# The first pair's Gram writes, its inverse's write and its first unit's read-back are begun by ScalarE instead of SyncE

## The chip, the core and the metric

The kernel runs on one core of a Trainium2 chip. The core has a matrix engine (TensorE, PE in the profile, with PEld for its weight loads), a vector engine (VectorE, DVE), an engine for activations and copies (ScalarE, ACT), a general engine (GpSimd, POOL) and an engine that only starts transfers (SyncE, SP). Transfers between the memory outside the core (DRAM in what follows) and the core's own memory are DMAs. SP, ACT and POOL can begin one; in the profile the queues of those engines are SPq, ACTq and POOLq. Every engine works through its own list of instructions in order.

The metric is the time of one execution on the device in microseconds (us), the median over runs.

## What is computed

Two stages run one after the other. The first is a recurrence over 768 time steps for 4 batches and 8 heads with vectors of 48 elements; the second is a layer with a cosine gate on the 3072 x 384 result.

```python
k_n = k / (np.linalg.norm(k, axis=-1, keepdims=True) + 1e-06)
state = np.zeros((B, H, D, D))
for t in range(S):
    y[:, :, t] = einsum('bhd,bhde->bhe', q[:, :, t], state)
    v_old = einsum('bhde,bhd->bhe', state, k_n[:, :, t])
    state = state + beta[:, :, t] * einsum('bhd,bhe->bhde', k_n[:, :, t], v[:, :, t] - v_old)
x = y.transpose(0, 2, 1, 3).reshape(B * S, H * D)      # 3072 x 384
h = x @ w_in                                           # w_in 384 x 2048
out = (h * cos(h)) @ w_out                             # w_out 2048 x 384
```

The reference's w_in and w_out are handed over in double precision; the kernel makes float32 of them itself.

## The kernel before

**Units and pairs.** The 768 steps are cut into 24 units of 32 steps (`NU`, `C`). Within a unit the recurrence is solved at once: a Gram matrix of the keys is formed for each batch and head (32 x 32), a triangular matrix made from it is inverted, and the inverse is applied to v less what the state already yields. Two units make a pair, m = 0 to 11, since 2 units x 8 heads x 4 batches = 64 matrices, each split in two shares, fill the 128 partitions for the inversion.

**The path of one pair.** For a unit n, PE transposes k and q (`turn`, tile p_t), ACT copies the result to kq_t (`turn_out`, L572), PE forms the Gram products p_g (`gram`, L593), and DVE scales the half that holds the keys into g (`gram_keys`, L604) and masks the other into tt (L613). `gram_put` (L620 to L633) writes g to DRAM as g_dr, one DMA for each of the first 8 units, three for later ones. When both units of a pair are written, `gram_get` (L640) reads them back in another layout as gb. `invert` (L669 and L676, one pair of instructions for a column) computes the inverse z: for pair 0 on DVE in a tile of the matrix engine's output memory, for all later pairs on POOL. For pair 0 ACT copies it out (`invert_out`, L680). `put` (L683 to L687) writes z to DRAM as z_dr, in 128-byte rows, and `get` (L689 to L694) reads it back for one unit as zt with four DMAs, one for each batch.

**Use of the inverse.** PE multiplies zt with the right side (`solve`, L742, p_u), DVE scales the result to u (`solve_out`, L752), PE forms the update of the state from u (`update`, L765, p_s), DVE adds it to the state st (L775 for unit 0, L773 later), and PE forms the unit's output (`within`, L782) and the products of the next unit with the state (`through_state`, L711). ACT copies the output to y (L793), PE transposes it (p_z, L801), ACT copies it to x_ffn (L809). Then the second stage runs on it: `hidden` (L822), later `layer` (L938), the gate on ACT and DVE, and `output` or `product` (L964, L1021).

**Weights.** w_in comes in 12 tiles, w_out in 16. Each is loaded by SP as pairs of 32-bit words (L462, tile pairs, 512 or 384 KB), split on ACT (L470 and L472), shifted on DVE (L476 and L481) and added on POOL (L485). The text counts the tiles t0, t1 and so on in the order of loading; t0 to t11 are those of w_in. The first hidden products need t0 to t2, the fourth t9 to t11. Further work on DVE that the text names: `norms_sum` (L502), `scale` (L525 to L533, after POOL's pow, L514), `weigh` (L550, the tile vp that holds v), `in_sums` (L915), `right_side` (L726, rhs).

**Order.** The order of the work is not that of the source. A planner, class `Order`, takes every task with an engine, an estimated cost, its dependences and a due time, plays the schedule through, and writes the instructions down in that order; at the end of the function each instruction is pinned behind the one before it on its engine. A task is planned on the engine that its entry names: `gram_put`, `put` and `get` are entered as tasks of SP, whoever begins the DMA in the end.

**Waits of DMAs.** The compiled program has eight completion semaphores for the DMAs that SP and ACT begin. They are handed out in turn over both engines' DMAs in the planner's order, and a DMA waits until the one that had the same semaphore before it has landed.

Of the kernel before, what the change touches and what calls it, by code (L numbers as in the profile page):

```python
# [248 lines left out]
def kernel(  # L249
# [32 lines left out]
    nc = tc.nc  # L282
# [31 lines left out]
    def half(i):  # L314
        return slice(DP * i, DP * i + DP)
# [4 lines left out]
    def quarter(b):  # L320
        return slice(C * b, C * b + C)
# [78 lines left out]
    for b in range(B):  # L400
        nc.gpsimd.dma_start(
            out=bq[C * b : C * b + H].rearrange("p n t -> p (n t)"), in_=beta[b]
# [80 lines left out]
    def narrow_add(t):  # L483
# [4 lines left out]
    sums, squares, scales, kq_ts, p_ts, p_gs, gs, grams, gbs, z_drs, zs, zts = (  # L488
        {} for _ in range(12)
    )  # L490
# [129 lines left out]
    def gram_put(n):  # L620
        m = n // 2
        if m not in gbs:
            gbs[m] = dram.tile([2, H, B, C, C], FP, name="g_dr")
        g, g_dr = gs.pop(n), gbs[m][n % 2]
        parts = [(slice(0, 128), slice(0, H), slice(0, B))]
        if n >= PLAIN_TURNS:
            parts = [(slice(0, 128), slice(0, H, 2), slice(0, B))] + [
                (half(i), slice(1, H, 2), slice(2 - 2 * i, 4 - 2 * i)) for i in range(2)
            ]
        for rows, heads, bs in parts:  # L630
            nc.sync.dma_start(
                out=g_dr[heads, bs].rearrange("h b j i -> (b j) h i"), in_=g[rows, heads]
            )  # L633

# [47 lines left out]

    def put(m):  # L683
        z_drs[m] = dram.tile([ROWS, SPLIT, 2, H, B, C], FP, name="z_dr")
        nc.sync.dma_start(
            out=z_drs[m].rearrange("r s u h b i -> (s u h b) r i"), in_=zs.pop(m)
        )  # L687

    def get(n):  # L689

        zts[n] = work.tile([128, H, C], FP, name="zt")
        z_dr = z_drs[n // 2].rearrange("r s u h b i -> u b (r s) h i")[n % 2]
        for b in range(B):
            nc.sync.dma_start(out=zts[n][quarter(b)], in_=z_dr[b])  # L694


    p_kqs, rhss, p_us, us, p_ss, ys, p_zs = ({} for _ in range(7))
# [407 lines left out]
    def inverse(m):  # L1105
        add(("gram_get", m), "SP", 1.2, lambda: gram_get(m),
            [("gram_put", 2 * m), ("gram_put", 2 * m + 1)], makes=[("gb", ("gb", m))],
            uses=[("g_dr", m)], moves=1.6)
        held = VECTOR.get(m)
        z = ("p_i", m) if held else ("z", m)  # L1110
        add(("eye", m), "ACT", 0.65, lambda: invert_eye(m, held),
            [("gram_put", 2 * m + 1)] + ([("eye", m - 1)] if m else []),
            makes=[(held or "z", z)])
        deps = [("eye", m), ("gram_get", m)]
        ends = [0, 4, 8, 12, 16, 20, 24, C - 1]
        for i, (x, y) in enumerate(zip(ends, ends[1:])):
            each = (0.2, 0.001) if held else (0.323, 0.00178)
            cost = sum(
                2 * (each[0] + each[1] * (j // SPLIT + 1) * (C - 1 - j)) for j in range(x, y)
            )  # L1120
            add(("inv", m, i), "DVE" if held else "POOL", cost,
                lambda x=x, y=y: invert(m, held, range(x, y)), deps,
                uses=[("gb", m)] if y == C - 1 else [])
            deps = [("inv", m, i)]
        if held:
            add(("inv_out", m), "ACT", 0.65, lambda: invert_out(m), deps,
                makes=[("z", ("z", m))], uses=[z])
            deps = [("inv_out", m)]
        add(("put", m), "SP", 0.45, lambda: put(m), deps, makes=[("z_dr", ("z_dr", m))],
            uses=[("z", m)], moves=1.7)  # L1130

    def unit(n):
# [47 lines left out]
        else:  # L1180
# [15 lines left out]
        add(("gram_queries", n), "DVE", 0.46, lambda: gram_queries(n), [("gram_keys", n)],  # L1196
            uses=[("p_g", n)])
        add(("gram_put", n), "SP", 0.45 if n < PLAIN_TURNS else 1.35, lambda: gram_put(n), [("gram_keys", n)],
            makes=[] if second else [("g_dr", ("g_dr", m))], uses=[("g_gram", n)],
            moves=0.85)  # L1200
        if second:
            inverse(m)
        add(("get", n), "SP", 1.9, lambda: get(n), [("put", m)], makes=[("zt", ("zt", n))],
            uses=[("z_dr", m)], moves=0.9)

# [275 lines left out]
```

## Time and profile before

| What | Value |
|---|---|
| time, median of 3 runs | 674.22 us (672.86 to 675.32) |
| the profiled execution, its own time | 676.74 us |
| its span, first to last instruction | 675.0 us |
| granted clock of TensorE | 0.99 |
| PE busy | 612.4 us (91%) |
| DVE busy | 475.6 us (70%) |
| POOL busy | 348.8 us (52%) |
| ACT busy | 295.5 us (44%) |
| DMA queue q1 (begun by SP) | 212964 packets, 49.98 MB, 39.0% of 16 engines |
| DMA queue q10 (begun by ACT) | 2176 packets, 0.39 MB, 0.4% |

The profile is one execution; its span is cut into 40 slices of 16.9 us for the rows of digits, in which 9 means busy for 90% or more. A line of a timeline gives the start in us from the start of the span, the duration, the engine, the line of the kernel, the operation, the tile written and the tile read, how many instructions are merged, and in brackets the idle time before it with what ended it. A line of waits gives who waited for whom, the sum in us, how often, and the longest. The chain of waits is followed back from the last instruction to what released each. In this kernel the chain runs through PE for 85% of the span, through DMA and POOL for 4% each.

### The profile page before, as it was taken

What the parts mean: (1) busy time and instruction counts of PE and PEld (TensorE: products, weight loads), DVE (VectorE), ACT (ScalarE), POOL (GpSimd) and SP (SyncE); (2) the same over time, 40 slices, a digit from 0 to 9 for tenths busy, and PEclk for the clock granted to TensorE, in tenths of its full rate; (3) what the DMA queues carried; (4) which work ended last, traced back from release to release, by engine and by line L of the source; (5) the groups of instructions that cost most, each with busy time, mean ns of one, the idle gap of its engine ahead of it and who ended that gap; (6) DMA issues with size and microseconds to landing.
All of it is one profiled execution on the core that took longest, in us unless ns stands there. A gap on an engine that the chain in (4) does not pass through costs nothing.

```text
span 675.0 us, 27309 instructions
## 1 busy us (share of the span) xinstructions
PE 612.4 (91%) x11864; PEld 573.0 (85%) x11864; DVE 475.6 (70%) x912; ACT 295.5 (44%) x510; POOL 348.8 (52%) x734
## 2 busy tenths in 40 slices
PE   4303798999999999999999999999999999999996
PEld 3203787896899989999999999999999989999996
DVE  5899488877576776886876876776766656656661
ACT  4432367572144452653543453544444434435530
POOL 4469888876858317678276384482382680000000
PEclk9999798999999999999999999999999999999999
DMA  8897766365462362443534524515213203000000
GB/s 179 193 197 169 165 141 166 84 104 90 68 100 54 58 106 52 71 82 59 110 42 62 108 39 66 106 26 90 57 21 53 59 3 57 1 5 24 1 24 24
DMA packets 215516, 52.56 MB, mean 78 GB/s; under 512 B 206948, under 2 KB 210164, under 8 KB 215396
## 3 DMA queue, kind: packets, MB, share of 16 engines
q1 hardware_dynamic: 212964, 49.98, 39.0%
q8 instruction: 93, 1.52, 1.0%
q10 hardware_dynamic: 2176, 0.39, 0.4%
q0 software_dynamic: 256, 0.44, 0.3%
q14 instruction: 27, 0.22, 0.1%
HBM read 39.76 MB, written 11.01 MB: 75 GB/s over the span
## 4 chain that ended last, share of the span: by engine, by line
PE 85%; DMA 4%; POOL 4%; issue 3%; SPq 2%; ACT 1%; DVE 1%; ACTq 0%; POOLq 0%; DVEq 0%
PE p_h L938 29%; PE p_out L1021 28%; PE p_h L822 6%; PE p_kq L711 4%; PE p_u L742 3%; PE p_s L765 3%; PE p_out L964 3%; PE p_kq L782 3%; PE p_g L593 2%; DMA kp<-in_k_dram 2%; PE p_o L1021 2%; PE p_z L801 1%; POOL knrm L514 1%; POOL w_in L485 1%; POOL part L669 1%
## 5 line engine op out<-in xcount | busy, mean ns | idle before, releaser
L669 POOL TENSOR_TENSOR part<-z,gb 128x126 f32<-128x126 f32 (+22 forms) x341 | 135.5, 397 | 109.4 <-DMA gb<-g_dr 44.9
L676 POOL TENSOR_TENSOR z<-z,part 128x126 f32<-128x126 f32 (+22 forms) x341 | 138.6, 406 | 26.7
L938 PE MATMUL p_h<-x_ffn,w_in 128*128 128x128 f32 x1120 | 143.6, 277 | 0.2 <-DVE g_ffn L957 0.2
L938 PEld LDWEIGHTS p_h<-x_ffn,w_in 128*128 128x128 f32 x1120 | 135.3, 192 | 1.9 <-DVE g_ffn L957 0.5
L1021 PE MATMUL p_out<-w_out,g_ffn 128*128 128x192 f32 x672 | 123.6, 329 | 1.6 <-issue 1.6
L1021 PEld LDWEIGHTS p_out<-w_out,g_ffn 128*128 128x128 f32 x672 | 107.6, 190 | 2.8 <-issue 1.7
L862 ACT ACTIVATE turns<-p_h 128x512 int32<-128x512 f32 x96 | 57.0, 595 | 101.3 <-DVE p_h L957 73.5
L1021 PE MATMUL p_out<-w_sum,g_ffn 128*128 128x192 f32 x496 | 91.6, 329 | 0.0
L874 ACT ACTIVATE turns<-turns 128x512 f32<-128x512 f32 x96 | 60.4, 630 | 46.2 <-DVE turns L867 46.1
L1021 PEld LDWEIGHTS p_out<-w_sum,g_ffn 128*128 128x128 f32 x496 | 79.3, 190 | 0.9
L867 DVE SCALAR_TENSOR_TENSOR turns<-p_h,turns 128x512 f32<-128x512 f32 x96 | 65.6, 684 | 17.6 <-ACT turns L862 17.2
L878 DVE TENSOR_TENSOR g_ffn<-turns,p_h 128x512 f32<-128x512 f32 x96 | 65.4, 681 | 17.9 <-ACT turns L875 17.0
L1037 DVE TENSOR_TENSOR g_ffn<-g_ffn 128x512 f32<-128x512 f32 x88 | 63.2, 719 | 13.2 <-PE p_out L1021 12.6
L514 POOL TENSOR_TENSOR knrm<-ksum,halves 128x16 f32<-128x16 f32 (+1 forms) x14 | 36.7, 2628 | 65.9 <-DVE ksum L502 65.9
L875 ACT ACTIVATE turns<-turns,halfpi 128x512 f32<-128x512 f32 x96 | 69.3, 722 | 3.1
L957 DVE TENSOR_TENSOR p_h<-g_ffn,p_h 128x512 f32<-128x512 f32 x60 | 41.7, 696 | 38.7 <-PE p_h L938 34.2
L954 ACT COPY g_ffn<-p_h 128x512 f32<-128x512 f32 x60 | 35.0, 583 | 74.2 <-PE p_h L938 73.9
L822 PE MATMUL p_h<-x_ffn,w_in 128*128 128x128 f32 x384 | 47.9, 283 | 0.6 <-POOL w_in L485 0.6
L822 PEld LDWEIGHTS p_h<-x_ffn,w_in 128*128 128x128 f32 x384 | 45.5, 196 | 2.0 <-POOL w_in L485 0.8
L1071 DVE SCALAR_TENSOR_TENSOR o<-p_out,o 128x192 f32<-128x192 f32 x74 | 25.2, 353 | 27.6 <-PE p_out L1021 25.2
L938 PE MATMUL p_h<-x_sum,in_sum 128*128 128x128 f32 x320 | 43.7, 280 | 0.0
L938 PEld LDWEIGHTS p_h<-x_sum,in_sum 128*128 128x128 f32 x320 | 39.5, 191 | 1.1
(95 smaller groups left out, 783.7 us busy)
## 6 DMA issues: line engine op xcount, KB each, us to landing
pairs<-in_moe_w_in_dram SPq DMA_DIRECT2D x12, 512.0 KB
gb<-g_dr SPq DMA_DIRECT2D x24, 256.0 KB
pairs<-in_moe_w_out_dram SPq DMA_DIRECT2D x16, 384.0 KB
vp<-in_v_dram SPq DMA_DIRECT2D x96, 48.0 KB
out_dram<-o SPq DMA_DIRECT2D x23, 192.0 KB
z_dr<-z SPq DMA_DIRECT2D x12, 256.0 KB
zt<-z_dr SPq DMA_DIRECT2D x96, 32.0 KB
kp<-in_k_dram SPq DMA_DIRECT2D x128, 24.0 KB
```

The costliest lines, as they stand in the source:

```text
L514: nc.gpsimd.tensor_tensor(out=scales[m][2][:, part], in0=sums[m, part.start][:, 0:n], in1=halves[:, 0:n], op=ALU.pow,)
L669: eng.tensor_tensor(out=part, in0=z[:, 0:rows, j, None].to_broadcast(shape), in1=a[:, j, None, j + 1 :].to_broadcast(shape), op=ALU.mult,)
L676: eng.tensor_tensor(out=behind, in0=behind, in1=part, op=ALU.subtract)
L822: nc.tensor.matmul(p_h[:, i], w_in[:, t, (4 * k + i) * 128 : (4 * k + i + 1) * 128], xts[p][:, t, unit * 128 : (unit + 1) * 128], start=(t ...
L862: nc.scalar.activation(turns[p, f], hidden_of(p, f), AF.Copy, scale=TURN)
L867: nc.vector.scalar_tensor_tensor(out=r, in0=hidden_of(p, f), scalar=TURN, in1=t, op0=ALU.mult, op1=ALU.subtract,)
L874: nc.scalar.activation(r, r, AF.Abs)
L875: nc.scalar.activation(r, r, AF.Sin, bias=halfpi, scale=-2.0 * math.pi)
L878: nc.vector.tensor_tensor(out=place(p, f), in0=step_of(rests.pop((p, f)), f), in1=step_of(hidden_of(p, f), f), op=ALU.mult,)
L938: nc.tensor.matmul(p_h[:, e], in_sum[:, odd_tile, 4 * s + e] if a == "s" else w_in[:, a, f * 128 : (f + 1) * 128], x_sums[p][:, unit] if b ...
L1021: nc.tensor.matmul(p_o, left(p, part, a)[:, e % 4], right(e, b), start=(e == 0), stop=(e == FT // 2 - 1), skip_group_check=True,)
L1037: nc.vector.tensor_tensor(out=left(p, s, to), in0=left(p, s, one), in1=left(p, s, two), op=op)
```

## The change

Three calls that began a DMA on SyncE begin it on ScalarE where the pair is the first (m is 0) or, for the read-back, where the unit is the first (n is 0). These are seven DMAs: g of units 0 and 1 (128 KB each), z of pair 0 (256 KB), and zt of unit 0 (four of 32 KB). The read of gb, the read-back for unit 1 and all later pairs stay on SyncE.

```diff
@@ gram_put @@
         for rows, heads, bs in parts:
-            nc.sync.dma_start(
+            (nc.sync if m else nc.scalar).dma_start(
                 out=g_dr[heads, bs].rearrange("h b j i -> (b j) h i"), in_=g[rows, heads]
             )
@@ put @@
         z_drs[m] = dram.tile([ROWS, SPLIT, 2, H, B, C], FP, name="z_dr")
-        nc.sync.dma_start(
+        (nc.sync if m else nc.scalar).dma_start(
             out=z_drs[m].rearrange("r s u h b i -> (s u h b) r i"), in_=zs.pop(m)
         )
@@ get @@
         for b in range(B):
-            nc.sync.dma_start(out=zts[n][quarter(b)], in_=z_dr[b])
+            (nc.sync if n else nc.scalar).dma_start(out=zts[n][quarter(b)], in_=z_dr[b])
```

The planner's entries are unchanged, so the order of PE, DVE and POOL stays as it was. On ACT the seven DMAs stand at the places that the planner's order gives them:

| ACT's list, after | Then |
|---|---|
| split of t1 (L470, L472) | g_dr of unit 0, then the two copies to kq_t of unit 2 (L572), then g_dr of unit 1, then ksq (L497) |
| split of t7 | z_dr |
| split of t8 | the four zt of unit 0, then the split of t9 |

On SP they are gone from between the other DMAs, which keep their order. The semaphores are handed out anew over the planner's order: z_dr has the place between the third and the fourth of the k loads that SP begins at 43.80 us, and the four zt stand between the q and v loads that SP begins at 49.35 and 53.84 us.

## Prediction

> **What bounds the kernel now.** First the page: the span and the row of TensorE (PE) by slices of 16.9 us.
>
> ```profile
> span 675.0 us, 27309 instructions
> ...
> PE   4303798999999999999999999999999999999996
> ...
> DMA  8897766365462362443534524515213203000000
> ```
>
> From about 75 us on PE is full, so only the moment at which it starts its dense part counts. PE is busy 612.4 us by the page; of its 62.6 idle us only about 7 lie after 75 us, by its waits. The waits of PE before 70 us name the last obstacle, and those from 75 to 130 us show how little slack comes after it:
>
> ```profile
> PE p_u L742 <- DMA zt<-z_dr: 25.4, 1, 25.4
> ...
> PE p_h L822 <- POOL w_in L485: 0.6, 1, 0.6
> ```
>
> PE waits 25.4 us for zt of unit 0, the read-back of the first pair's inverse. The timeline of SyncE's queue (SP) shows how that read comes about:
>
> ```profile
> 48.38 0.39 SPq L462 DMA_DIRECT2D pairs<-in_moe_w_in_dram  x1
> 48.87 0.39 SPq L685 DMA_DIRECT2D z_dr<-z  x1
> 49.35 4.45 SPq L369 DMA_DIRECT2D qp<-in_q_dram  x4
> 53.84 1.93 SPq L369 DMA_DIRECT2D vp<-in_v_dram  x4
> 55.87 0.39 SPq L462 DMA_DIRECT2D pairs<-in_moe_w_in_dram  x1
> 56.31 4.13 SPq L694 DMA_DIRECT2D zt<-z_dr  x8
> 60.54 0.40 SPq L462 DMA_DIRECT2D pairs<-in_moe_w_in_dram  x1
> ```
>
> By the landing events of the trace the write of z_dr lands at 54.06, yet zt is begun at 56.31: SP has four q loads, four v loads and a weight load to issue first. The first four zt land at 60.40 to 60.95. So far an earlier zt looks like a gain of 3 us. VectorE (DVE) says otherwise, because the step after p_u is its u (L752):
>
> ```profile
> 59.91 0.68 DVE L915 TENSOR_TENSOR in_sum<-w_in 128x512 f32<-128x512 f32 x1
> 61.40 0.69 DVE L476 SCALAR_TENSOR_TENSOR pairs<-pairs 128x512 uint32<-128x512 uint32 x1 [0.81 <-ACT pairs L472]
> 62.01 0.42 DVE L481 TENSOR_SCALAR w_in<-w_in 128x512 uint32<-128x512 uint32 x1
> 62.51 1.02 DVE L752 TENSOR_TENSOR u<-p_u,bz 128x384 f32<-128x384 f32 x2
> ```
>
> In DVE's order the shift of weight tile t9 stands ahead of u and ends at 62.43, while p_u ends at 62.47: two chains arrive together. The shift waits for ScalarE (ACT), and ACT for the weight load that SP began at 55.87 and that landed at 60.13:
>
> ```profile
> 47.47 0.69 ACT L470 ACTIVATE w_in<-pairs 128x512 f32<-128x512 f32 x1 [1.33 <-DMA pairs<-in_moe_w_in_dram]
> ...
> 52.48 0.67 ACT L470 ACTIVATE w_in<-pairs 128x512 f32<-128x512 f32 x1 [3.75 <-DMA pairs<-in_moe_w_in_dram]
> ...
> 60.15 0.67 ACT L470 ACTIVATE w_in<-pairs 128x512 f32<-128x512 f32 x1 [6.45 <-DMA pairs<-in_moe_w_in_dram]
> ```
>
> One more thing is needed, the waits of SP's queue from 44 to 66 us:
>
> ```profile
> SPq L694 <- DMA pairs<-in_moe_w_in_dram: 0.4, 1, 0.4
> ```
>
> A read of zt waits for a weight load with which it shares no data. It is the eighth zt, the eighth DMA after that load: begun at 60.14, 0.01 after the load landed. Eight completion semaphores are handed round over all DMAs of SP and ACT together, and each DMA waits until the one eight places ahead has landed. I call them lanes.
>
> **What the Trainium skill says.** "DMA: Bandwidth & Descriptors", Issuing engines are not separate DMA queues: all issuers share the same 16 DMA engines, so a second issuer saves issue time only. The trace bears on this with DMA busy 7 to 9 tenths until 84 us. Queues, rings and completion order there gives SP and ACT a ring each, served in turn by packets: a write on ACT's ring need not stand behind SP's loads. No run here shows how the two share. Anatomy of one DMA adds that semaphores are waited for on the issuing sequencer, before dispatch; the eighth zt agrees, and SP's next load at 60.54 stood behind it.
>
> **The change part by part.** It moves 7 DMA issues (two g_dr, one z_dr, four zt of unit 0) from SP to ACT; no arithmetic changes.
>
> *Gram writes.* On SP they took 0.40 and 0.54 us at 17.79 and 18.29. On ACT one stands ahead of the copies of kq_t at 17.05, one behind them; ACT's q loads at the start took 0.32 to 0.47 us each, so about 0.9 us is added there. Behind them is ksq at 18.22, which DVE reads at 19.91; it ended at 18.74, so 1.17 us of slack cover the 0.9. If that failed, the pow of POOL at 20.53 and everything behind it would slip by the rest. The lanes move too: one write takes a place ahead of the last k load of unit 3, one ahead of its q loads, so the last three q loads wait for lanes that land at 15.90, 16.23 and 17.71, and the third weight load begins about 18.1 instead of 16.95. It lands 1.2 us later; the fourth unit's Gram product follows at about 24.2 to 25.4, and its consumer on DVE stands at 25.86: covered by 0.4. The read gb waits for both writes; on their own ring they land earlier than 22.39, but 1 MB of weights still stands ahead of gb. I take DVE's inverse to start at 27.4 as now, between 0.4 earlier (DVE is free at 26.95) and 1 us later; later it is hidden by the 0.81 us that DVE waits at 60.6 and by the point below. Cost 0, bounds 0 and +1.
>
> *Write of z.* z is ready on ACT at 46.15, but the issue stands behind the split that runs 47.47 to 48.73: begun at 48.75, against 48.87. Landing: now 54.06 behind a weight load; a z_dr issued alone at 237.34 took 3.26 us. So 52.0 to 54.1; I take 53.3. SP loses an issue and the stall of 2.97 us that its next q load shows at 49.35, but the second of those q loads (52.37 now) has the lane that z_dr holds, eight places on: it waits until 53.3.
>
> *Reads of zt.* On ACT behind the split of tile t8: load landed 52.45, split ended 53.71. So zt is begun at 53.8, 54.25, 54.7, 55.2. Undisturbed zt take 1.8 to 2.0 us (at 202 to 205 us); they land at 55.8, 56.3, 56.8, 57.3, some 3.6 us earlier than now, and p_u ends near 59.3.
>
> *What is late next.* SP now issues the q load at 53.3, its next at 53.7, 54.15, then v at 54.65; the second v waits for the q load of 53.3 to land (55.4), the third at 55.8, the fourth for the first zt (56.2), and the load of t9 for the second zt, eight places ahead: about 56.6 instead of 55.87. A weight load takes 3.9 to 4.3 us (4.25 for this one): landed at 60.8, +0.7. Split, shift and u follow with the same gaps as now (60.13 to 62.51, 2.38): u at 63.2, +0.7. p_u is long done. DVE's earlier wait for v (weighing at 57.92, its last v landed at 57.55, then at 58.5) ends 0.6 later and fits in the wait ahead of the shift.
>
> *To the end.* p_s follows u by 1.17; state, features and the first hidden product (75.18) follow without a wait on anything that stands still: the gap of 2.94 at 68.48 is an issue gap inside PE and moves along. POOL's 0.6 at 91 depends on weight loads that SP issues after v of the next pair, which wait for DVE's rhs, so it moves too. The whole 0.7 reaches the end. Span 675.0 + 0.7 = 675.7; with the 1.74 outside it (676.74 less 675.0) 677.4 for a profiled execution. That one lay 2.5 above the median of 674.22; on the median the forecast is 674.9.
>
> **The rivals.**
> A. No harm at t9, and the early zt counts (0.08). Then DVE is free at 60.59, its shift ends at 61.6, u at 61.7: at most 0.8 gained, 673.4. For it: p_u no longer holds u. Against: t9's lane. To beat 0.3% (2.02 us; about what this measurement can tell from no change) something else must help too, such as two fuller rings in the first 50 us; 0.06.
> B. Slower (0.27): the two rings share the engines between 48.8 and 54, so the load of t8, now landed ahead of z_dr, lands up to 1.5 later, at 54. ACT's split stands ahead of zt and ends at 55.3; the second zt lands at 57.8, t9 begins at 58, lands at 62.2, u is 2.1 late: 676.3, with the zt themselves at 3 us 677.4. It decides above 0.3% from a second zt landing after 57.8. For it: DMA busy 9 and 7 tenths in the slices to 50.6 and 67.5 us. Against: the load is issued 0.4 ahead of z_dr.
> C. The Gram writes cost more (inside B's chance for a third): an issue of over 0.6 us each on ACT, or gb over 1.9 later; +1 to +2 on its own, 675.5 to 676.5.
> D. That nothing happens, since the reads land too late in either kernel: ruled out by the order on ACT, which leaves zt over 2 us earlier.
>
> **How the numbers follow.** The forecast (t9 later by 0.3 to 1.6) has 0.6, A 0.08, B and C 0.27, a clear gain 0.05. Predicted 674.9; the forecast's own range with the spread of the median, 0.8, is 673.8 to 676.4. To leave no more than 2 in 10 out, 673.0 to 677.6. Faster 0.06, same 0.65, slower 0.29.
>
> **What would show it.** In the changed profile: ACT issues g_dr near 17.1 and 18.5, z_dr near 48.8, four zt from 53.8; PE's p_u begins between 55.8 and 57.4; its wait for DVE's u grows from 1.2 to about 4; t9 begins at 56.3 to 57.5 and ACT splits it at 60.5 to 61.5; the first hidden product starts near 75.9. Wrong if u stays at 62.5 or earlier, if gb on DVE starts after 28.5, or if the gap at 68.48 vanishes.

## The result, and the profile after

Over 12 runs each, the changed kernel took 675.24 us (median, 672.37 to 680.11) and the kernel before 675.09 us (671.92 to 678.81). The ratio is 1.0003, its 95% interval 0.9978 to 1.0028: no difference that can be measured. Run again beside the experiments below, it was 1.0008 (0.9985 to 1.0031). Of all timed executions here one, of r6 below, took 1710.73 us and does not count in its ratio.

The page of the changed kernel, span and rows by slices of 16.8 us:

```profile
span 672.6 us, 27309 instructions
...
PE   4302898999999999999999999999999999999996
...
PEclk9999699999999999999999999999999999999999
```

PE becomes dense in the same slice as before, the fifth. The timeline of the queues and of ACT shows the moved DMAs where the prediction had put them:

```profile
48.33 0.67 ACT L470 ACTIVATE w_in<-pairs 128x512 f32<-128x512 f32 x1 [1.70 <-DMA pairs<-in_moe_w_in_dram]
48.39 0.39 ACTq L685 DMA_DIRECT2D z_dr<-z  x1
48.89 0.66 ACT L472 ACTIVATE pairs<-pairs 128x512 uint32<-128x512 uint32 x1
49.23 0.40 SPq L462 DMA_DIRECT2D pairs<-in_moe_w_in_dram  x1
49.73 4.05 SPq L369 DMA_DIRECT2D qp<-in_q_dram  x4
53.96 3.20 SPq L369 DMA_DIRECT2D vp<-in_v_dram  x4
53.97 0.67 ACT L470 ACTIVATE w_in<-pairs 128x512 f32<-128x512 f32 x1 [4.42 <-DMA pairs<-in_moe_w_in_dram]
54.03 0.83 ACTq L694 DMA_DIRECT2D zt<-z_dr  x2
54.53 0.66 ACT L472 ACTIVATE pairs<-pairs 128x512 uint32<-128x512 uint32 x1
54.90 0.96 ACTq L694 DMA_DIRECT2D zt<-z_dr  x2
...
57.44 0.35 SPq L462 DMA_DIRECT2D pairs<-in_moe_w_in_dram  x1
```

The read-back of zt begins at 54.03 instead of 56.31, and t9's load (the last line) at 57.44 instead of 55.87. The waits of SP's queue from 44 to 60 us say why t9's load is later:

```profile
SPq L369 <- DMA z_dr<-z: 2.0, 1, 2.0
SPq L369 <- DMA zt<-z_dr: 1.6, 1, 1.6
...
SPq L462 <- DMA zt<-z_dr: 0.2, 1, 0.2
```

A q load waits for z_dr, a v load for the first zt, t9's load for the second zt. None shares data with what it waits for; they share completion semaphores, handed round over SP's and ACT's DMAs together. VectorE's timeline shows the end of that chain, and PE's waits what it costs there:

```profile
62.71 0.69 DVE L476 SCALAR_TENSOR_TENSOR pairs<-pairs 128x512 uint32<-128x512 uint32 x1 [1.24 <-ACT pairs L472]
63.32 0.42 DVE L481 TENSOR_SCALAR w_in<-w_in 128x512 uint32<-128x512 uint32 x1
63.65 1.01 DVE L752 TENSOR_TENSOR u<-p_u,bz 128x384 f32<-128x384 f32 x2
```

```profile
PE p_s L765 <- DVE knrm L525: 5.4, 1, 5.4
```

The profile names the instruction next to u on DVE as the releaser; in r4 below it names u. Of that wait at most 1.24 us, the idle time ahead of the shift, is due to t9's load; most of the rest is DVE's own work, as r5 and r8 below show. p_u now starts at 56.97 and ends near 59.4, and PE then stands 5.4 us until u is there (1.2 before). The early read-back bought a longer wait.

### The profile page after: what moved, and what is told of

Read it like the earlier page. It is cut to its first block, busy times and chain, and to the rows that moved or that the text cites. A ratio compares the mean times of both kernels' runs of the same rounds, so it can differ in the third digit from the quotient of the medians.

```text
span 672.6 us, 27309 instructions
## 1 busy us (share of the span) xinstructions
PE 612.6 (91%) x11864; PEld 573.3 (85%) x11864; DVE 474.4 (71%) x912; ACT 295.5 (44%) x510; POOL 346.4 (52%) x734
## 3 DMA queue, kind: packets, MB, share of 16 engines
q10 hardware_dynamic: 7408, 1.05, 1.0%
q8 instruction: 93, 1.52, 1.0%
## 4 chain that ended last, share of the span: by engine, by line
PE 80%; DMA 8%; SPq 3%; POOL 2%; DVE 2%; issue 2%; ACT 1%; ACTq 0%; POOLq 0%
PE p_h L938 29%; PE p_out L1021 27%; PE p_h L822 5%; PE p_kq L711 4%; PE p_out L964 3%; PE p_s L765 3%; PE p_u L742 3%; PE p_kq L782 2%; PE p_g L593 2%; DMA pairs<-in_moe_w_in_dram 2%; POOL knrm L514 2%; DMA kp<-in_k_dram 2%; DMA zt<-z_dr 2%; PE p_o L1021 2%; DMA z_dr<-z 1%
## 5 line engine op out<-in xcount | busy, mean ns | idle before, releaser
L676 POOL TENSOR_TENSOR z<-z,part 128x126 f32<-128x126 f32 (+22 forms) x341 | 136.9, 402 | 26.7
L822 PE MATMUL p_h<-x_ffn,w_in 128*128 128x128 f32 x384 | 48.9, 288 | 0.4 <-issue 0.4
L822 PEld LDWEIGHTS p_h<-x_ffn,w_in 128*128 128x128 f32 x384 | 46.5, 201 | 1.7 <-POOL z L676 0.7
```

The lines of the kernel that those rows point to most:

```text
L676: eng.tensor_tensor(out=behind, in0=behind, in1=part, op=ALU.subtract)
L822: nc.tensor.matmul(p_h[:, i], w_in[:, t, (4 * k + i) * 128 : (4 * k + i + 1) * 128], xts[p][:, t, unit * 128 : (unit + 1) * 128], start=(t ...
```

## The experiments

All, r1 to r12 for short, compute the same. All but r4, r7 and r8 reorder the planner's tasks; r4 is the changed kernel as it is, r7 and r8 are the two parts of the change. The edit is nine lines in class `Order` and a table: a task named in the table is written only after the task it is held behind, and the rest keeps its order.

```diff
+    HOLD = {task: the task that it is held behind}
+    def write(self, key, emit, makes, wrote, seen=set(), held={}):
+        if self.HOLD.get(key, key) not in seen | {key}:
+            held.setdefault(self.HOLD[key], []).append((key, emit, makes))
+            return
+        emit()
+        wrote([tag for tag, _ in makes])
+        seen.add(key)
+        [self.write(k, e, t, wrote) for k, e, t in held.pop(key, ())]
...
-                emit()
-                wrote([tag for tag, _ in makes])
+                self.write(key, emit, makes, wrote)
```

One table of marks serves for all of them: one profiled execution of each kernel, us from the start of its span, and the ratio to the kernel before from timed runs made beside it. "t11 ready" is the end of t11's add on POOL (L485); the p_out is the first of L964; "later p_h" is the hidden product of L822 that comes first after the second group of p_out. An issue gap, in what follows, is idle time of an engine in which it waited for nothing that the profile shows.

| Kernel | u | first p_h | t11 ready | first p_out | later p_h | ratio (95%) |
|---|---|---|---|---|---|---|
| before | 62.51 | 75.18 | 90.98 | 93.69 | 117.75 | 1 |
| changed | 63.65 | 75.44 | 91.37 | 95.10 | 117.92 | 1.0003 (0.9978 to 1.0028) |
| r1 | 59.13 | 74.39 | 91.33 | 94.04 | 113.73 | 0.9981 (0.9964 to 0.9997) |
| r2 | 61.73 | 76.65 | 91.51 | 94.23 | 118.15 | 1.0033 (1.0017 to 1.0048) |
| r3 | 65.56 | 76.34 | 91.41 | 94.12 | 116.02 | 1.0030 (1.0013 to 1.0047) |
| r4 | 62.00 | 73.43 | 89.57 | 92.63 | 115.42 | 1.0008 (0.9985 to 1.0031) |
| r5 | 60.81 | 75.75 | 90.86 | 93.92 | 117.39 | 1.0016 (0.9997 to 1.0035) |
| r6 | 61.95 | 75.46 | 90.61 | 93.58 | 115.82 | 1.0007 (0.9980 to 1.0034) |
| r7 | 62.69 | 75.49 | 91.27 | 93.99 | 117.85 | 1.0014 (0.9997 to 1.0032) |
| r8 | 62.36 | 73.67 | 90.13 | 92.84 | 115.46 | 1.0011 (0.9995 to 1.0028) |
| r9 | 61.93 | 77.21 | 93.33 | 96.22 | 117.67 | 1.0029 (1.0014 to 1.0045) |
| r10 | 61.06 | 72.52 | 90.44 | 93.16 | 115.25 | 1.0016 (0.9991 to 1.0040) |
| r11 | 61.60 | 74.88 | 90.36 | 93.07 | 115.08 | 1.0000 (0.9983 to 1.0018) |
| r12 | 58.42 | 73.32 | 86.57 | 92.98 | 115.63 | 1.0004 (0.9986 to 1.0023) |

**r1 and r2: does what stands ahead of u eat the early zt?** On DVE, the weighing of v, the copies of beta, in_sum, the shift of t9 and a scale go behind the copy of st (`update_out`), and on PE a Gram product goes later; r2 is the same on the kernel before.

```diff
+    HOLD = {("weigh", 1): ("update_out", 0), ("beta_home",): ("update_out", 0), ("in_sums", 3, 0): ("update_out", 0),
+            ("shift", 9): ("update_out", 0), ("scale", 2, 0): ("update_out", 0), ("gram", 4): ("state", 1)}
```

> The changed kernel, with u of unit 0 (and the state copy after it) taken ahead of the work that DVE had in front of it: the weighing of v, the copies of beta, in_sum, the shift of t9 and the scale of pair 2; on PE the Gram product of unit 4 goes behind the state product of unit 1. Theory (the early zt is lost because u stands behind the shift of t9, which waits for a weight load tied to the zt by the semaphores): u starts within 0.3 us of the end of p_u, at 59 to 60.5 instead of 63.65; the first hidden product starts near 72 instead of 75.4. Whether the end gains is then set by POOL: its adds of t6 to t11 end near 85 to 91 whatever PE does, so PE waits 2 to 4 us for w_in and at most 1.1 us reaches the end (about 674). Rival (nothing else holds PE back): the whole 3 to 3.5 us reach the end, about 671.5, with no wait of PE for POOL. Second rival (u was not held by t9): u stays later than 62.

> The same moves on DVE and PE in the kernel before, as the control. Theory: p_u ends at about 62.5 there, so u cannot start before and stays at 62.4 to 62.7; the first hidden product within 1 us of 75.2, the time within 0.3% of before. Rival (the moves themselves are worth something or cost something): over 2 us away from before in either direction.

With the list cleared, u follows p_u in the changed kernel by 0.03 us: 59.13, which is 4.5 us ahead of the changed kernel's first profile and 2.9 ahead of its second, r4. That half of the theory is shown. The first hidden product, expected near 72, gained only 1.05 us on the first profile and none on r4 (73.43). PE's waits of r1 from 40 to 140 us name what came instead:

```profile
PE p_kq L711 <- ACT y L793: 3.1, 1, 3.1
PE p_z L801 <- DVE tt L613: 2.1, 1, 2.1
PE p_h L822 <- POOL w_in L485: 1.9, 2, 1.2
PE p_s L765 <- DVE u L752: 1.2, 1, 1.2
```

ACT's copy of y stands behind the splits of t9 and t10 and a ksq; DVE's tt stands behind the work that was moved. The control r2 is slower by 0.33%, a little more than its theory allowed, so the moves cost time by themselves; r1 is 0.52% better than its control, and 0.19% better than the kernel before.

**r3: is PE's dense part bound by u at all?** In the kernel before, zt of unit 0 is read only behind t10's load.

```diff
+    HOLD = {("get", 0): ("weights", 10)}
```

> The kernel before with the four reads of zt for unit 0 behind those for unit 1 and the load of t10 on SP. They are begun near 59 instead of 56.3 and land near 63 to 64; u starts near 65 instead of 62.5. Theory (from u on, nothing stands still that could take up a delay): the end comes 2 to 3 us later, about 677. Rival (a wait later on, such as POOL's adds, takes it up): within 1 us of before.

u came 3.05 us later and the first hidden product 1.2 later, since the issue gap on PE that was 2.94 us shrank to 0.88. t11 and the first p_out came 0.4 later. The timed runs lost 0.30%, 2.0 us, which fits the theory. That it was the lateness of u which reached the end is not shown: the profile loses most of it on the way, and r2 lost as much with u 0.8 earlier than in the kernel before.

**r4: the changed kernel again.**

> The changed kernel once more. Theory: t9's load on SP begins within 0.1 us of the landing of the second zt, SP's second q load of that group within 0.1 us of the landing of z_dr, u 0.5 to 1.5 us later than 62.5, and the time within 0.3% of before. Rival (the single profile was an accident): t9 begins before the second zt has landed, or u at 62.5 or earlier.

The waits are the same (p_s 5.3 us for u; SP 2.1 for z_dr, 1.2 and 0.2 for zt), yet u stands at 62.00 and the first hidden product at 73.43, 2.0 earlier than in the first profile of the same kernel. z was copied at 45.05 here, at 46.04 there: single executions of one kernel differ by a microsecond before the write of z and the reads of zt are even reached. By the rival (u at 62.5 or earlier), and by the prediction's own sign of being wrong, this execution speaks against a late u; the two waits through shared semaphores stand in it as forecast.

**r5 and r6: t9's load alone.** The four q loads ahead of t9's load are begun behind it; r6 is the kernel before with the same edit.

```diff
+    HOLD = {("q", 6): ("weights", 9)}
```

> The changed kernel with one edit on SP: the four q loads that stood ahead of the four v loads and of t9's load are begun behind t9's load. PE, DVE, ACT and POOL keep their order, u still stands behind the shift of t9. Theory (the late load of t9 on SP is what eats the early zt): t9's load is begun near 53.5 instead of 57.4 and lands near 57.5 to 58; its split on ACT ends near 59.2, its shift on DVE near 60.2, so u starts near 60.2 to 60.6 instead of 62.0 to 63.65, PE's wait for u falls from 5.3 to about 2, and two thirds of some 2.5 us reach the end: ratio 0.9975 (0.9965 to 0.9985). Rival (DVE's own list, the weighing and in_sum, holds u, or the traffic of q behind t9 slows the read-back): u stays at 61.5 or later, ratio 0.999 to 1.002.

> The kernel before with the same edit on SP, as a control. Theory: t9's shift is then early (near 60), but the read-back of zt keeps its place behind v, t9 and q on SP, p_u ends near 62.5 as before, and u follows it: ratio 1.000 (0.9985 to 1.0015). Rival (an early t9 is worth something by itself, through POOL's adds or SP's later loads): ratio below 0.9985.

u moved to 60.81 in r5, as the theory said, and the wait ahead of t9's shift (1.24 us in the changed kernel, 0.89 in r4) is gone. But the rival is right in part. PE's wait for u fell to 2.07, but at least half of that because p_u ended later, 15.09 us after the start of z's copy (13.37 in the changed kernel, 12.81 in r4); and no wait was left ahead of u on DVE from z's copy on, yet u came 16.0 us after it. The same holds for r8 below, in which t9's load was not moved and PE waited 5.0 us for u. VectorE's timeline of r8 has no bracket ahead of u, so no wait:

```profile
60.82 0.68 DVE L915 TENSOR_TENSOR in_sum<-w_in 128x512 f32<-128x512 f32 x1
61.42 0.69 DVE L476 SCALAR_TENSOR_TENSOR pairs<-pairs 128x512 uint32<-128x512 uint32 x1
62.02 0.42 DVE L481 TENSOR_SCALAR w_in<-w_in 128x512 uint32<-128x512 uint32 x1
62.36 1.02 DVE L752 TENSOR_TENSOR u<-p_u,bz 128x384 f32<-128x384 f32 x2
```

So DVE's own work between z's copy and u takes some 16 us (15.7 to 16.2 in the six profiles without a wait there: r5, r6 and r8 to r11), and t9's load only adds its wait to that. r1, which takes work away, has 13.2.

The time of r5 did not follow (1.0016; the control 1.0007). In its timelines of SP, ACT and PE:

```profile
60.16 1.47 SPq L462 DMA_DIRECT2D pairs<-in_moe_w_in_dram  x1
...
65.59 0.68 ACT L470 ACTIVATE w_in<-pairs 128x512 f32<-128x512 f32 x1 [7.53 <-DMA pairs<-in_moe_w_in_dram]
...
67.67 0.46 ACT L793 COPY y<-p_kq 128x384 f32<-128x384 f32 x1
...
68.18 1.79 PE L711 MATMUL p_kq<-st,kq_t 48*32 48x48 f32 x128 [1.31 <-ACT y L793]
```

What was taken from t9 was given to t10: its load ended late, ACT split it at 65.59, and y, behind that split, held PE. A further issue gap of 3.41 us stood ahead of the second p_u.

**r7 and r8: the change in its two parts,** the Gram writes alone and the rest alone.

```diff
-            nc.sync.dma_start(
+            (nc.sync if m else nc.scalar).dma_start(
                 out=g_dr[heads, bs].rearrange("h b j i -> (b j) h i"), in_=g[rows, heads]
```

This is r7, against the kernel before; r8 has the two other parts of the change's diff and not this one.

> The kernel before with only the two Gram writes of the first pair on ACT. Theory (this part costs nothing and gives nothing that lasts): gb on DVE is read between 26.9 and 28.4, the later chain stands as before, zt on SP near 56.3, u near 62.5; ratio 1.000 (0.9985 to 1.0015). Rival 1 (the late third and fourth weight loads push the inverse): DVE's inverse starts at 28 or later and all behind it moves by 0.7 to 1: ratio 1.001 to 1.0015. Rival 2 (the writes on their own ring bring gb early): inverse starts at 26.9, ratio 0.999 to 0.9995.

> The kernel before with only the write of z and the read-back of unit 0 on ACT, the Gram writes on SP. Theory (all that the change does about u is in this part): zt begun near 53.5 on ACT, p_u from 55.5 to 57, t9's load begun 0.7 to 1.2 later than 55.87, u at 62.3 to 63.6 behind t9's shift, PE waits 5 us for u: ratio 1.000 (0.999 to 1.0015). Rival (the Gram part had cost what this part gave): u at 61.7 or earlier, ratio 0.997 to 0.9985.

In r7 DVE's inverse started at 27.76 after a wait of 0.50 for gb (27.38 and 0.44 before) and u at 62.69; in r8 zt was begun at 53.12, t9's load at 56.35, u at 62.36, with 5.0 us of PE's wait for it. Neither ratio differs from 1 or from the other's: no large gain in one part is hidden by a loss in the other.

**r9, r10, r11: the walls behind u.** r9 is r5 with y ahead of t10's split; r10 clears the path of units 0 and 1 on all engines; r11 is r10's control, on the kernel before.

```diff
+    HOLD = {("q", 6): ("weights", 9), ("split", 10): ("within_out", 0), ("square", 3, 0): ("within_out", 0), ("shift", 10): ("split", 10)}
```

```diff
+    HOLD = {("q", 6): ("weights", 9), ("split", 10): ("within_out", 0), ("square", 3, 0): ("within_out", 0), ("shift", 10): ("right", 1),
+            ("sum", 3, 0): ("right", 1), ("scale", 2, 0): ("update_out", 0), ("gram", 4): ("features_out", 0), ("gram_keys", 4): ("gram", 4),
+            ("gram_queries", 4): ("gram_keys", 4), ("gram_put", 4): ("gram_keys", 4), ("split", 11): ("features_out", 0), ("shift", 11): ("split", 11),
+            ("inv", 1, 6): ("add", 8), ("put", 1): ("inv", 1, 6), ("add", 12): ("add", 10), ("add", 13): ("add", 12)}
```

> The changed kernel with t9's load ahead of the q loads (as in r5_after_t9_early) and, on ACT, y of unit 0 ahead of the split of t10 and the ksq behind it. Theory (in r5_after_t9_early the wall behind u was t10's load, which began 1.5 late and held y in ACT's list): u near 60.8, y near 65.1 instead of 67.67, PE's wait for y (1.31) gone, the p_kq of unit 1 near 66.9 instead of 68.18, the first hidden product 1.3 earlier than 75.75, ratio 0.9985 to 1.000. Rival (the issue gap of 3.41 inside PE takes up what comes early): first hidden product at 75.3 or later, ratio as in r5_after_t9_early, 1.001 to 1.002.

> r9_after_y_first, and further moves on the path of units 0 and 1: on DVE st of unit 0 ahead of the scale of pair 2, rhs of unit 1 ahead of the shift of t10; on PE gram of unit 4 behind p_z; on ACT the split of t11 behind x_ffn; on POOL the adds of t7 and t8 ahead of the last part of pair 1's inverse, and those of t9 and t10 ahead of the first two of w_out. Theory (each of these stood on the path behind the early zt): u near 60.8, p_kq of unit 1 near 65.6, rhs near 67.4, first hidden product between 71 and 74 (70.9 and an issue gap), no wait for POOL's w_in above 0.5; ratio 0.995 to 0.998. Rival (POOL is the bound behind it: the later z_dr of pair 1, or w_in's adds, take the gain back between 80 and 100 us): first hidden product at 72 to 74, new waits of PE of 2 us or more on POOL or on zt of unit 2, ratio 0.9985 to 1.002.

> The kernel before with the same moves as r10_after_full, as its control. Theory (the early zt is worth its time only where nothing stands behind it): p_u ends near 62.5 and u follows at once, so every step to the first hidden product is 1.7 to 2 later than in r10_after_full; ratio 0.15 to 0.3 per cent above that of r10_after_full. Rival (an issue gap of PE or POOL's work sets the start of the dense part in either kernel): both ratios agree within 0.1 per cent.

r9 is a miss of the theory: PE's wait for y vanished, but issue gaps of 2.27 and 3.03 us stood in its place, the first hidden product came at 77.21, and the ratio is 1.0029. r10's first hidden product came where the theory had it, at 72.52, 2.4 ahead of its control, but not through u: 0.9 of the 2.4 stands already at z's copy (44.90 and 45.80), 1.46 is an issue gap that the control has just before 71.41 and r10 lacks, and counted from z's copy u is no earlier (16.16 and 15.80). The timed runs do not bear the theory out: the control was to be slower by 0.15% to 0.3% and measured 1.0000 against 1.0016. And r10's first p_out stands at 93.16, the control's at 93.07. Ahead of it lie, in r10's timeline of PE,

```profile
81.95 0.89 PE L765 MATMUL p_s<-u,kp 64*64 64x96 f32 x32 [1.71 <-ACT kq_t L572]
...
90.49 2.50 PE L822 MATMUL p_h<-x_ffn,w_in 128*128 128x128 f32 x20 [1.06 <-POOL w_in L485]
```

and the second is the more general. In r10 t11 was ready at 90.44, and PE started at 90.49. The same pair of rows in the kernel before, first PE's timeline, then POOL's:

```profile
91.03 2.50 PE L822 MATMUL p_h<-x_ffn,w_in 128*128 128x128 f32 x20 [0.64 <-POOL w_in L485]
```

```profile
89.36 1.62 POOL L485 TENSOR_TENSOR w_in<-w_in,pairs 128x512 uint32<-128x512 uint32 x1
```

89.36 and 1.62 make 90.98; PE started 0.05 later. In ten of the kernels (before, r1, r2, r3, r5, r7 to r11) this product began 0.05 to 0.06 us after t11 was ready, with the first hidden product anywhere from 72.5 to 77.2. PE waited only 0.2 to 1.1 us there, r10 1.06 where its control waited 0.27. POOL was busy for 9.9 to 10.0 of the 11 us from 80 to 91 in before, r1 and r10, mostly on adds. Its list is a second clock that u doesn't set: counted from z's copy, u comes after 13.2 us in r1, 17.0 in the kernel before and 19.8 in r3, and t11 is ready after 45.4, 45.4 and 45.6.

**r12: take that wall away,** in the kernel that was fastest. r1 with the adds of three tiles of w_out behind the add of t11.

```diff
+            ("add", 12): ("add", 11), ("add", 13): ("add", 11), ("add", 14): ("add", 11)}
```

> r1_after_u_early with one edit more, on POOL: the adds of the first three tiles of w_out stand behind the add of t11 instead of between the adds of t7 to t11. Theory (the first hidden products need t9 to t11 at about 90 us whatever comes before, and in nearly every kernel the fourth of them starts within 0.06 us of the end of t11's add on POOL, so POOL's list is what eats an earlier start): t11's add ends near 87.5 instead of 91.3, both waits of PE for POOL's w_in (1.22 and 0.64 in r1_after_u_early) vanish, the first p_out starts near 92.3 instead of 94.04, ratio 0.9955 (0.994 to 0.997). Rival (the next wall stands directly behind it: the adds of w_out, that p_out needs, end as late as before, or DVE's turns and rhs come no earlier): p_out at 93.5 or later, ratio 0.9975 to 0.999.

POOL's timeline, then PE's, of r12:

```profile
79.44 7.13 POOL L485 TENSOR_TENSOR w_in<-w_in,pairs 128x512 uint32<-128x512 uint32 x5
86.53 3.40 POOL L485 TENSOR_TENSOR w_out<-w_out,pairs 128x384 uint32<-128x384 uint32 x3
```

```profile
87.58 1.22 PE L711 MATMUL p_kq<-st,kq_t 48*32 48x48 f32 x110 [0.86 <-issue]
...
92.62 0.52 PE L801 MATMUL p_z<-consts,y 128*128 128x128 f32 x3 [0.49 <-DVE tt L613]
92.98 2.75 PE L964 MATMUL p_out<-w_out,g_ffn 128*128 128x384 f32 x8
```

t11 was ready at 86.57, 4.8 us earlier than in r1, and both waits for POOL are gone, as the theory said. The first p_out gained 1.06 over r1, but this execution's first hidden product was 1.07 earlier already: issue gaps and DVE's tt stand where POOL's waits (1.86 us together) were. The ratio is 1.0004, so for the time the theory falls. In this profile the rival's picture fits, a next wall directly behind POOL's, though its numbers (p_out at 93.5 or later, a ratio below 1) were not met.

**Where r1's profile gains.** At its first p_out, r1 is 0.35 later than the kernel before, so the lead of its profile does not come from the early u as such. It comes between 107 and 114 us. PE's timelines, the kernel before, then r1:

```profile
109.12 0.66 PE L562 MATMUL p_t<-consts,kp 128*128 128x128 f32 x4
112.08 1.02 PE L562 MATMUL p_t<-consts,qp 128*128 128x128 f32 x4 [2.30 <-issue]
112.89 4.12 PE L964 MATMUL p_out<-w_out,g_ffn 128*128 128x384 f32 x8
```

```profile
109.31 0.66 PE L562 MATMUL p_t<-consts,kp 128*128 128x128 f32 x4
109.80 0.60 PE L562 MATMUL p_t<-consts,qp 128*128 128x128 f32 x4
110.24 2.75 PE L964 MATMUL p_out<-w_out,g_ffn 128*128 128x384 f32 x8
```

All other profiles have an issue gap of 0.7 to 2.3 us among these transposes; r1 has none. In the kernel before the clock was halved after it as well: eight p_out took 4.12 us instead of 2.75. Why r1 lacks the gap is open, and r12, which differs from r1 on POOL alone, has it again (1.66). Nor does the gap explain r1's ratio: the two spans lie 4.7 us apart, the medians beside each other 1.6 (672.05 and 673.67), and r3, r6 and r8 have spans as short (670.5 to 671.1) and ratios above 1. r1 is the only kernel here that measured below the kernel before, by 0.03% to 0.36%. Among thirteen such ratios one that narrow can be chance; that it would repeat was not tried, and its cause stays open.

## Why the prediction was right

**Gram writes, cost 0.** Right as to the cost. ACT issued them at 16.62 and 17.58 (near 17.1 and 18.5 forecast), 0.41 and 0.42 us each; DVE's inverse started at 27.87, 26.87 in r4, 27.0 to 28.4 being the bounds (r4 stays 0.1 below). r7's ratio, 1.0014, can't tell a loss of 1 us from none; its profile shows none of C's conditions. The forecast took no gain here, though it saw room for one, and the profiles suggest one: in all six with the Gram writes on SP, gb landed at 27.3 to 28.5 and DVE waited 0.44 to 1.72 us for it ahead of the inverse; in the eight with them on ACT, gb landed at 25.6 to 27.6 and DVE waited 0.48 to 0.66 in three (r1, r7, r9) and not at all in five. z's copy came 18.2 us behind the start of the inverse in each. None of it shows in the timed runs.

**Write of z.** Begun at 48.39 (48.75 forecast). SP's second q load waited for its semaphore until 52.47, so it had landed by then: 0.8 earlier than taken, inside the bounds.

**Reads of zt.** At 54.03 (53.8), p_u at 56.97 (55.8 to 57.4): right, by two errors that cancelled. The step took t8's load as undisturbed. It came 1.5 late, as rival B had it, 0.85 because it was begun later and 0.64 because it took longer (49.23 to 53.97, against 48.38 to 52.48, the end taken at the split's start). And the step put the issue behind the end of the split; it was begun 0.06 us after the split's first instruction began, ahead of its second. That is why B's price did not come with B's mechanism. The Trainium skill, "Perfetto Trace Analysis", DVE / Act Engine Instruction, has a sequencer that goes on to the next instruction once it has pushed one into the wait queue, which fits: z_dr shows the same 0.06.

**t9's load and u, +0.7.** That t9's load waits for the second zt, eight places on, is shown by SP's waits above, and that u's shift can wait for that load by the brackets ahead of it. What the step had wrong is the weight of it: t9's load adds a wait of 0.71 to 1.24 us or none, and DVE's own list, with 16 us from z's copy to u, keeps u late without it (r5, r8). The size is not firm. Counted from the start of z's copy, which clears away what differs between executions before it (and the Gram writes' gain with it), u came after 16.95 us before (62.51 less 45.56), 17.61 in the changed kernel, 16.95 in r4 and 15.87 in r8. So the term is +0.7 in one execution, 0 and -1.1 in the others. From the span's start u stood at 62.00 in r4 and 62.36 in r8, where the prediction calls itself wrong at 62.5 or earlier.

**To the end.** Here a step failed: "The whole 0.7 reaches the end", with the gap of 2.94 moving along and POOL's 0.6 at 91 moving too. The issue gap does not move along: it was 2.19 in the changed kernel, 1.50 in r4, 0.88 in r3. And POOL's wait is not behind u: in r1 and r3 u moved by 3 us and more, and t11 was ready 0.35 and 0.43 us later than in the kernel before. Starts of the dense part 4 us apart end in first p_outs within 1.6 us of each other (92.6 to 94.2), leaving out r9 and the changed kernel's first profile, whose clock stayed at half until 80 and 82 us. So the forecast had the right sum, near zero, and the wrong reason at its end: not +0.7 carried through, but a small shift of u, of either sign, that later waits absorb. That part of its success is luck, and the timed runs could not have told: 0.7 us is 0.10%, inside the interval from -0.22% to +0.28%. Whether a shift of 3 us is absorbed as well stays open (r3).

**The rivals.** A (the early zt counts where t9 does no harm) was tried in r5 and r10: u came early in both, the first hidden product in r10 alone, the time in neither. A's sum, at most 0.8 us for u because DVE's list ends no earlier, agrees with the 15.7 to 16.2 us above. C asked for issues of over 0.6 us or a gb over 1.9 later, and r7 shows 0.41 and DVE's start 0.4 later.

## What to carry to other kernels

Before an early transfer is counted as a gain, list everything in program order ahead of its consumer on the consumer's engine, what those wait for, and how long they take with no wait at all (here some 16 us from z's copy to u); then do the same for the next engine, until a wait appears that the change does not reach (here POOL's add at 91 us). A DMA moved to another issuing engine can still hold the first engine's DMAs through a shared completion semaphore, so count the places. And where executions of one kernel differ by several microseconds, compare marks along the path counted from a common event, not spans.

## What the hardware showed beyond this

The granted clock of TensorE changes in steps of 3.41 us. The record of the trace has, in us from the span's start and without the halved end of each execution, from 667 us or later:

```
changed kernel  half from 72.04 to 82.28 (3 steps)
before          half from 71.28 to 78.11 (2 steps), and from 112.24 to 115.65 (1 step)
r1              full from 76.69 to 667.19
```

The Trainium skill, "TensorE: Matmul & The Clock Gate", Part 1: The HAM clock gate, gives a free-running window of 4096 cycles at 1.2 GHz, 3413 ns, after which an idle engine is throttled to half. The trace agrees on the length of the window. It does not show that the window has to be idle throughout: near 112 us, in before, r2, r5 and r7, PE was busy for 1.10 to 1.52 us of the 3.41 ahead of the half-speed step, and where it was busy for 1.58 or more in its window there, in the other ten profiles, the clock stayed full. Busy time is not the whole rule either: r5 has one more such step, at 248.15, with 2.31 us busy ahead of it.

What that does here: before, r2, r5 and r7, with their step near 112 us, have spans of 673.9 to 675.7; r1, r3, r6, r8, r10, r11 and r12 have none between 80 us and the end, and lie at 670.3 to 671.3 us. The groups follow the step and not the kernel, so a single profiled span can't rank these kernels; the timed runs of one kernel spread over as much. But the step is not the only cause. By an estimate from its length, 3.41 us at half speed cost at most 1.7, and the groups lie at least 2.6 apart; and the changed kernel, r4 and r9, without it, have 672.5 to 673.1.
